# Clustered attention with two MLP layers: exponentials kept in PSUM, fp16 halves made from there, one more buffer each, a lag of three

## The chip, the cores and the metric

The kernel runs on one core of one Trainium2 chip. The metric is device time in microseconds (us), the median of several runs; less is better. Times of single steps come from one profiled execution.

## The reference

Attention in which a query sees only the keys of its own cluster, then two dense layers. Everything is fp32; the core of it:

```python
q_assign = np.argmax(np.einsum('bhsd,hcd->bhsc', q_n, c_n), axis=-1)
k_assign = np.argmax(np.einsum('bhsd,hcd->bhsc', k_n, c_n), axis=-1)
mask = q_assign[:, :, :, None] == k_assign[:, :, None, :]
scores = scale * np.matmul(q, k.transpose(0, 1, 3, 2))
scores = np.where(mask, scores, -1000000000.0)
attn = np.exp(scores - np.max(scores, axis=-1, keepdims=True))
attn = attn / (np.sum(attn, axis=-1, keepdims=True) + 1e-09)
x = np.matmul(attn, v)          # then (B * S, H * D)
h = x @ w1_in;  x = (h * (1.0 / (1.0 + np.exp(-h)))) @ w1_out
h = x @ w2_in;  out = (np.maximum(h, 0.0) + alpha * np.minimum(h, 0.0)) @ w2_out
```

The sizes: batch 2, 8 heads, 768 positions, head width 64, 16 clusters; 1536 tokens, model width 512, inner width 2048.

## The kernel before, in words

**Number format.** Matmuls run in fp16 with three products each: every operand is a sum of a high and a low fp16 half (hi x hi, hi x lo, lo x hi). So each intermediate is split into two halves by a copy to fp16 and a subtraction. The same holds for the weights W1 and W2 (layer 1 and layer 2, each with an `in` and an `out` matrix), which arrive as 64-bit floats, are rebuilt as fp32 from their two 32-bit words and then scaled and split (`to_f32`, `split`, lines 566 to 609), in pieces of 1 MB, on VectorE, ScalarE and GpSimd together.

**Units.** Attention is cut into 96 units: 12 tiles of 128 query rows times 8 heads. Unit `u` has two parts. `front(u)` (line 448) makes the scores of one head for 128 rows against 768 keys: four TensorE matmuls (L458 for the cluster mask, L462 for q times k) into one PSUM score tile `s` of two banks; there are two such tiles (`ps_s`, bufs=2). VectorE takes the row maximum (L474) and two tiny steps (L477, L478). ScalarE takes the exponential with the row sum (L480) into an SBUF buffer `p` of fp32 (a ring of two, `p_buf`), copies it to the high fp16 half (L487), and VectorE subtracts to get the low half (L489). `front_t(u)` (line 493) issues a DMA transpose (L495) of both halves from SyncE's queue (two buffers of halves, `o_hl`; three of transposed halves, `o_pt`, `NPT`). `back(u)` (line 497) multiplies the transposed halves by V: 18 short TensorE matmuls (L507) that add into the PSUM tile `x`, which holds all heads of a query tile. When a tile's eight heads are done, `x_done` (line 520) normalizes, splits and transposes it (L538).

**Order of the work.** `attention()` (line 719) is a generator that emits unit after unit: `front(u)`, then `back(u - LAG)` with `LAG = 2`, then `front_t(u)`, and between them preparation of the next tile's queries (`prep_q_a`, `prep_q_b`), of the second batch's keys and values (from unit 40 on), and background tasks that convert W1. Layer 1 (`layer1`, line 804) runs in seven chunks of one or two tiles. For each chunk the generator is advanced to the unit in `UNITS_BY_CHUNK = (32, 53, 64, 69, 98, 98, 98)` in equal steps between layer 1's steps: 16 first-product groups (L834: 12 matmuls, then tanh L840, L841, copy L844, subtraction L845) and 16 second-product groups (L865). When the generator has made all `NU + LAG` steps, `w2_start` emits the loads and conversions of W2, which reuse the memory of the keys, values and attention buffers. Layer 2 (`layer2`, line 929; L937, L946, L947, L950, L951, L968) follows in three column blocks. A list scheduler then decides the order of each engine's instructions from these priorities, from dependences and from free buffers, so the order below is not simply the program text. Each engine runs its own queue strictly in that order.

The lines of the loop that the change touches:

```python
o = p_buf()
nc.scalar.activation(
    out=view(o, F32, 2, hs), in_=sc[:, :, :hs], func=ACTF.Exp, scale=scl, bias=bias,
    accum_out=sums[n % 2][:, h:h + 1],
)
p = view(o, F32, S)
hl = view(o_hl + 3 * KB * i, F16, 2, S)
nc.scalar.activation(out=hl[:, 0], in_=p, func=ACTF.Copy)
```

The names in rows: `arena` is the one SBUF region in which nearly everything lies, `s` a score tile, `x` the attention output in PSUM, `w` and `m` PSUM tiles of the layers, `stat` small columns.

## Time and profile before

| | us |
|---|---|
| median of 3 runs | 877.86 |
| lowest and highest | 873.18, 877.96 |
| the profiled execution, own time | 873.64 |
| its span in the trace | 871.5 |
| TensorE busy (share of the span) | 704.7 (81%) |
| VectorE busy | 607.4 (70%) |
| ScalarE busy | 468.5 (54%) |
| GpSimd busy | 153.5 (18%) |

Engines in rows: PE is TensorE (PEld its weight loads), DVE VectorE, ACT ScalarE, POOL GpSimd, SP SyncE, which issues the DMAs. `L489` is line 489 of the kernel. Busy time counts an instruction's whole span; in the slices a digit is the busy share in tenths, one slice being a fortieth of the span. A wait is put down to the instruction whose end released it. PEclk is the granted share of TensorE's clock.

### The profile page before, as it was taken

How to read it: one execution, taken by the hardware profiler on the slowest of the kernel's cores; microseconds unless marked ns; L12 is line 12 of the kernel's file. 1: busy time of each engine (PE TensorE's matmuls, PEld its weight loads, DVE VectorE, ACT ScalarE, POOL GpSimd, SP SyncE). 2: the span in 40 equal slices, each digit the busy share in tenths (PEclk: the TensorE clock that was granted, in tenths of full speed). 3: DMA queues.
4: the chain of work that ended last, by engine and by line, in shares of the span. 5: the costliest groups of instructions: out<-in, count | busy, mean ns of one | idle time of the engine just before them, and what ended most of it. 6: DMA issues, size and time to landing. Idle time of an engine off the chain costs nothing.

```text
span 871.5 us, 16209 instructions
## 1 busy us (share of the span) xinstructions
PE 704.7 (81%) x6484; PEld 487.1 (56%) x6484; DVE 607.4 (70%) x1302; ACT 468.5 (54%) x861; POOL 153.5 (18%) x117
## 2 busy tenths in 40 slices
PE   2435267777887997899898869789969999999998
PEld 1323146675766776788677758667424444444443
DVE  6999988888967777875986777786993058206700
ACT  7837576647857664755765577868541023002200
POOL 5734520340201220000000004341190000000000
PEclk9995567689999999999999999999999999999999
DMA  9999878659896786784778687353100000000000
GB/s 278 235 229 249 252 177 134 122 118 163 143 173 115 119 166 98 138 140 73 123 123 139 118 222 177 116 201 139 48 1 13 24 13 1 13 25 12 1 25 25
DMA packets 241595, 101.86 MB, mean 117 GB/s; under 512 B 217328, under 2 KB 227568, under 8 KB 241392
## 3 DMA queue, kind: packets, MB, share of 16 engines
q1 hardware_dynamic: 241520, 100.83, 54.0%
q8 instruction: 51, 0.84, 0.4%
q14 instruction: 24, 0.20, 0.1%
HBM read 44.08 MB, written 3.15 MB: 54 GB/s over the span
## 4 chain that ended last, share of the span: by engine, by line
PE 36%; DMA 12%; DVE 10%; ACT 4%; issue 2%; POOL 1%; SPq 0%; POOLq 0%; DVEq 0%; ACTq 0%
PE w L968 10%; DMA arena<-arena 8%; PE w L937 6%; PE m L968 5%; PE m L937 4%; PE w L865 3%; PE w L834 3%; DMA arena<-in_moe_w_out_dram 2%; PE x L507 2%; DMA arena<-in_moe_w_in_dram 2%; DVE arena L583 1%; DVE arena L586 1%; PE s L458 1%; PE s L462 1%; DVE arena L951 1%
## 5 line engine op out<-in xcount | busy, mean ns | idle before, releaser
L834 PEld LDWEIGHTS <-arena 128*128 128x128 f16 x1344 | 126.6, 107 | 35.1 <-issue 18.8
L834 PE MATMUL w<-arena 128*128 128x256 f16 (+1 forms) x1212 | 137.5, 273 | 10.6 <-DVE arena L841 8.5
L507 PE MATMUL x<-arena 128*128 128x64 f16 x1728 | 75.0, 202 | 79.9 <-DMA arena<-arena 78.9
L865 PEld LDWEIGHTS <-arena 128*128 128x128 f16 x1344 | 118.5, 100 | 20.7 <-POOL arena L605 2.9
L865 PE MATMUL w<-arena 128*128 128x256 f16 (+1 forms) x1200 | 123.9, 260 | 5.4 <-POOL arena L605 2.5
L507 PEld LDWEIGHTS <-arena 128*128 128x128 f16 x1728 | 66.2, 104 | 95.4 <-DMA arena<-arena 91.8
L489 DVE TENSOR_TENSOR arena<-arena 128x768 f16<-128x768 f32 x96 | 95.0, 991 | 32.3 <-ACT arena L487 32.0
L474 DVE TENSOR_REDUCE stat<-s 128x1 f32<-128x768 f32 x96 | 91.1, 951 | 28.4 <-PE s L462 28.2
L480 ACT ACTIVATE arena<-s,stat 128x768 f32<-128x768 f32 x96 | 94.5, 985 | 26.3 <-DVE stat L478 25.5
L487 ACT ACTIVATE arena<-arena 128x768 f16<-128x768 f32 x96 | 80.5, 842 | 42.0 <-DMA arena<-arena 41.0
L937 PEld LDWEIGHTS <-arena 128*128 128x128 f16 x576 | 57.0, 99 | 80.0 <-issue 15.5
L968 PEld LDWEIGHTS <-arena 128*128 128x128 f16 x576 | 56.4, 98 | 68.0
L580 POOL TENSOR_SCALAR arena<-arena 128x1024 f32<-128x1024 f32 x28 | 43.2, 1541 | 287.2 <-DMA arena<-in_moe_w_in_dram 219.1
L937 PE MATMUL w<-arena 128*128 128x512 f16 x384 | 87.7, 383 | 5.3 <-DVE arena L947 5.3
L458 PE MATMUL s<-arena 80*128 80x384 f16 x192 | 69.8, 364 | 17.6 <-DMA arena<-arena 11.1
L968 PE MATMUL w<-arena 128*128 128x512 f16 x384 | 83.9, 379 | 0.0
L950 ACT ACTIVATE arena<-arena,stat 128x512 f16<-128x512 f32 x48 | 34.5, 720 | 88.2 <-DVE arena L947 86.2
L462 PE MATMUL s<-arena 128*128 128x384 f16 x192 | 69.8, 364 | 0.0
L840 ACT ACTIVATE arena<-w,stat 128x256 f32<-128x256 f32 (+1 forms) x101 | 43.5, 434 | 29.3 <-PE w L834 24.2
L583 DVE SCALAR_TENSOR_TENSOR arena<-arena 128x1024 int32<-128x1024 int32 x32 | 42.9, 1340 | 22.1 <-ACT arena L572 8.3
L946 DVE TENSOR_SCALAR arena<-w,stat 128x512 f32<-128x512 f32 x32 | 24.0, 749 | 46.9 <-PE w L937 46.5
L845 DVE SCALAR_TENSOR_TENSOR arena<-arena 128x256 f16<-128x256 f32 (+1 forms) x112 | 49.7, 451 | 6.0 <-ACT arena L844 5.9
(137 smaller groups left out, 1014.1 us busy)
## 6 DMA issues: line engine op xcount, KB each, us to landing
arena<-in_moe_w_in_dram SPq DMA_DIRECT2D x16, 1024.0 KB, 5.9
arena<-in_moe_w_out_dram SPq DMA_DIRECT2D x16, 1024.0 KB, 5.1
arena<-in_k_dram SPq DMA_DIRECT2D x8, 384.0 KB, 3.8
arena<-in_q_dram SPq DMA_DIRECT2D x6, 512.0 KB, 4.9
arena<-in_v_dram SPq DMA_DIRECT2D x8, 384.0 KB, 5.8
out_dram<-arena SPq DMA_DIRECT2D x12, 256.0 KB, 2.0
arena<-arena SPq DMA_TRANSPOSE x149, 3.9
arena<-in_moe_alpha_dram SPq DMA_DIRECT2D x1, 1024.0 KB, 4.7
```

The source lines that it names most:

```text
L458: nc.tensor.matmul(out=sc[:, j, :hs], lhsT=qt2[0:D + C, h], rhs=kt2[0:D + C, h % 2, j * hs:(j + 1) * hs], start=True, stop=False,)
L462: nc.tensor.matmul(out=sc[:, j, :hs], lhsT=qt1[:, h], rhs=kt1[:, h % 2, j * hs:(j + 1) * hs], start=False, stop=True,)
L474: nc.vector.tensor_reduce(out=nm, in_=sc[:, :, :hs], axis=AX.XY, op=ALU.max, negate=True)
L480: nc.scalar.activation(out=view(o, F32, 2, hs), in_=sc[:, :, :hs], func=ACTF.Exp, scale=scl, bias=bias, accum_out=sums[n % 2][:, h:h + 1],)
L487: nc.scalar.activation(out=hl[:, 0], in_=p, func=ACTF.Copy)
L489: en.tensor_tensor(out=hl[:, 1], in0=p, in1=hl[:, 0], op=ALU.subtract)
L507: nc.tensor.matmul(out=x_ps[0][:, h], lhsT=pt[:, ph * T + t], rhs=vt[:, h % 2, t, vh], start=(i == 0), stop=(i == 3 * T - 1),)
L583: nc.vector.scalar_tensor_tensor(out=lo, in0=hi, scalar=3, in1=lo, op0=ALU.logical_shift_left, op1=ALU.bitwise_or)
L834: nc.tensor.matmul(out=hp, lhsT=wi[:, a, kd, f % 2 * 128:f % 2 * 128 + 128], rhs=mov(bb, kd), start=(i == 0), stop=(i == 3 * KD - 1),)
L865: nc.tensor.matmul(out=acc, lhsT=wo[:, a, f % 2, dt * 128:(dt + 1) * 128], rhs=g[:, f, bb], start=(i == 0), stop=(i == 3 * KF - 1),)
L937: nc.tensor.matmul(out=hp, lhsT=in_piece(o_a + 24 * KB, f // 2)[:, a, kd, f % 2 * 128:][:, :128], rhs=x[bb][:, kd], start=(i == 0), stop=( ...
L968: nc.tensor.matmul(out=acc, lhsT=g[:, f, a, t * 128:(t + 1) * 128], rhs=out_piece(o_w, f // 2)[:, bb, f % 2], start=(i == 0), stop=(i == 3 ...
```

## The change

The exponential overwrites the scores in their PSUM tile; the ring `p` is gone. The copy to the high half and the subtraction for the low half read the exponentials from PSUM. The memory of `p` goes to a third buffer of halves (`NHL = 3`) and a fourth of transposed halves (`NPT = 4`). `LAG` is 3. The table `P_LO_DVE`, which had given every subtraction to VectorE, goes, and VectorE keeps them all. `UNITS_BY_CHUNK` stays, so its 98 is now one less than `NU + LAG`.

```diff
--- before.py
+++ after.py
@@ -37,7 +37,6 @@
 V_SCALE_ON = ("papa", "appp")
 SPLIT = ("dddddddd", "dddbdddb", "dbdbdbdb", "dccdcbbc")
 EXP_ON = ("pppppppp", "pppppppp", "appppapp", "papapppp")
-P_LO_DVE = range(96)
 
 MASK = 2.0 ** 15
 BIT23 = 2.0 ** 23
@@ -77,7 +76,8 @@
     NC2 = 3
     N2 = NTILE * 128 // NC2
 
-    NPT = 3
+    NPT = 4
+    NHL = 3
     NSTAT = 464
     NSCR = 192
 
@@ -124,8 +124,7 @@
     o_qraw = region(4 * KB)
     o_kvraw = region(8 * KB)
     o_preq = region(4 * KB)
-    o_p = region(6 * KB)
-    o_hl = region(6 * KB)
+    o_hl = region(NHL * 3 * KB)
     o_pt = region(NPT * 3 * KB)
     o_xf = region(2 * KB)
     o_xhl = region(2 * KB)
@@ -229,9 +228,6 @@
         i = ring_pos.get(name, 0)
         ring_pos[name] = i + 1
         return i % n
-
-    def p_buf():
-        return o_p + 3 * KB * ring("p", 2)
 
 
     half = small_p.tile([128, 12], F32, name="half")
@@ -476,22 +472,19 @@
         )
         nc.vector.tensor_scalar(scl, nm, 2.0 ** 29, d[:, pr:pr + 1], op0=ALU.is_lt, op1=ALU.mult)
         nc.vector.tensor_scalar(bias, nm, scl, None, op0=ALU.mult)
-        o = p_buf()
+        p = sc[:, :, :hs]
         nc.scalar.activation(
-            out=view(o, F32, 2, hs), in_=sc[:, :, :hs], func=ACTF.Exp, scale=scl, bias=bias,
+            out=p, in_=p, func=ACTF.Exp, scale=scl, bias=bias,
             accum_out=sums[n % 2][:, h:h + 1],
         )
-        p = view(o, F32, S)
-        i = u % 2
-        hl = view(o_hl + 3 * KB * i, F16, 2, S)
+        hl = view(o_hl + 3 * KB * (u % NHL), F16, 2, 2, hs)
         nc.scalar.activation(out=hl[:, 0], in_=p, func=ACTF.Copy)
-        en = nc.vector if u in P_LO_DVE else nc.gpsimd
-        en.tensor_tensor(out=hl[:, 1], in0=p, in1=hl[:, 0], op=ALU.subtract)
+        nc.vector.tensor_tensor(out=hl[:, 1], in0=p, in1=hl[:, 0], op=ALU.subtract)
         pt = view(o_pt + 3 * KB * (u % NPT), F16, 2 * T, 128)
         pt_of[u] = pt
 
     def front_t(u):
-        hl = view(o_hl + 3 * KB * (u % 2), F16, 2 * S)
+        hl = view(o_hl + 3 * KB * (u % NHL), F16, 2 * S)
         nc.sync.dma_start_transpose(out=pt_of[u], in_=hl)
 
     def back(u):
@@ -711,7 +704,7 @@
                 f()
 
 
-    LAG = 2
+    LAG = 3
     NU = NTILE * H
     ready = set()
     g1_done = set()
```

The scheduler gives another order. First VectorE late in attention, amid the first product of a layer-1 chunk, before: the subtractions (L489) of units 69 and 70 and the reductions (L474) of units 71 and 72.

```order
L841 SCALAR_TENSOR_TENSOR arena<-arena,w 128x256
L489 TENSOR_TENSOR arena<-arena 128x768
L474 TENSOR_REDUCE stat<-s 128x1
L416 SCALAR_TENSOR_TENSOR arena<-arena,stat 128x8x64
L423 COPY arena<-arena 128x8x64
L477 TENSOR_SCALAR stat<-stat 128x1
L841 SCALAR_TENSOR_TENSOR arena<-arena,w 128x256
L845 SCALAR_TENSOR_TENSOR arena<-arena 128x256
L474 TENSOR_REDUCE stat<-s 128x1
L478 TENSOR_SCALAR stat<-stat 128x1
L468 TENSOR_SCALAR stat<-stat 128x4
L489 TENSOR_TENSOR arena<-arena 128x768
```

Now, at the corresponding place: the subtractions of units 68 and 69 and the reduction of unit 70 (lines have moved: L470 is the reduction, L482 the subtraction, L834 and L838 the layer-1 pair, L473 and L474 the tiny steps).

```order
L482 TENSOR_TENSOR arena<-s,arena 128x768
L474 TENSOR_SCALAR stat<-stat 128x1
L834 SCALAR_TENSOR_TENSOR arena<-arena,w 128x256
L838 SCALAR_TENSOR_TENSOR arena<-arena 128x256
L470 TENSOR_REDUCE stat<-s 128x1
L838 SCALAR_TENSOR_TENSOR arena<-arena 128x256
L834 SCALAR_TENSOR_TENSOR arena<-arena,w 128x256
L473 TENSOR_SCALAR stat<-stat 128x1
L482 TENSOR_TENSOR arena<-s,arena 128x768
L474 TENSOR_SCALAR stat<-stat 128x1
L834 SCALAR_TENSOR_TENSOR arena<-arena,w 128x256
L838 SCALAR_TENSOR_TENSOR arena<-arena 128x256
```

Before, a subtraction stands behind the reduction of the unit two later; now behind that of the unit one later, and one reduction lies between two subtractions instead of two.

The second place is VectorE where the scale of W1's `out` matrix is set (L682; L675 now), which the first L865 waits for; these are the rows before it, before.

```order
L489 TENSOR_TENSOR arena<-arena 128x768
L164 TENSOR_SCALAR stat<-stat 128x1
L474 TENSOR_REDUCE stat<-s 128x1
L845 SCALAR_TENSOR_TENSOR arena<-arena 128x128
L167 TENSOR_SCALAR stat<-stat 128x1
L682 TENSOR_SCALAR stat<-stat 128x8
L477 TENSOR_SCALAR stat<-stat 128x1
L474 TENSOR_REDUCE stat<-s 128x1
```

And now.

```order
L470 TENSOR_REDUCE stat<-s 128x1
L280 TENSOR_SCALAR arena<-arena 128x8x16
L838 SCALAR_TENSOR_TENSOR arena<-arena 128x128
L473 TENSOR_SCALAR stat<-stat 128x1
L159 TENSOR_SCALAR stat<-w 128x1
L474 TENSOR_SCALAR stat<-stat 128x1
L163 TENSOR_SCALAR stat<-stat 128x1
L166 TENSOR_SCALAR stat<-stat 128x1
L482 TENSOR_TENSOR arena<-s,arena 128x768
L675 TENSOR_SCALAR stat<-stat 128x8
```

Before, it stands behind the reduction of unit 22 and the subtraction of unit 20; now behind the reduction of unit 17 and the subtraction of unit 16.

The third place is SyncE's queue at the end of attention: transposes of the last units (L495; L488 now), the last x (L538; L531), the loads of W2 (L561; L554) and of alpha (L889; L882), before.

```order
L538 DMA_TRANSPOSE arena<-arena 128x8x128
L561 DMA arena<-in_moe_w_in_dram 128x4x512
L495 DMA_TRANSPOSE arena<-arena 128x12x128 x2
L889 DMA arena<-in_moe_alpha_dram 128x2048
L561 DMA arena<-in_moe_w_in_dram 128x4x512
L495 DMA_TRANSPOSE arena<-arena 128x12x128 x2
L561 DMA arena<-in_moe_w_in_dram 128x4x512
L495 DMA_TRANSPOSE arena<-arena 128x12x128 x2
L561 DMA arena<-in_moe_w_in_dram 128x4x512
L538 DMA_TRANSPOSE arena<-arena 128x8x128
```

And now.

```order
L488 DMA_TRANSPOSE arena<-arena 128x12x128 x2
L554 DMA arena<-in_moe_w_in_dram 128x4x512
L488 DMA_TRANSPOSE arena<-arena 128x12x128 x2
L882 DMA arena<-in_moe_alpha_dram 128x2048
L554 DMA arena<-in_moe_w_in_dram 128x4x512
L488 DMA_TRANSPOSE arena<-arena 128x12x128
L554 DMA arena<-in_moe_w_in_dram 128x4x512
L488 DMA_TRANSPOSE arena<-arena 128x12x128
L531 DMA_TRANSPOSE arena<-arena 128x8x128
L554 DMA arena<-in_moe_w_in_dram 128x4x512 x5
```

Six unit transposes stand behind the first W2 load before, four now; the loads of W2 stand among them in both.

## Rows read from the trace of the kernel before

**Rows 1.** The page, busy tenths in 40 slices of the span, two engines.
```profile
PE   2435267777887997899898869789969999999998
...
DVE  6999988888967777875986777786993058206700
```

**Rows 2.** Busy time by stretch; columns in the first line.
```profile
core 0: us, PE busy (x) PEld busy (x) DVE busy (x) ACT busy (x) POOL busy (x), PEclk, DMA share, GB/s
50.00:168.00 118.00, 65.51 (x715) 51.17 (x716) 107.52 (x241) 76.13 (x140) 34.61 (x20) 0.68 0.90 205
168.00:508.00 340.00, 288.41 (x3708) 239.56 (x3706) 262.54 (x652) 219.36 (x438) 35.77 (x23) 0.96 0.74 129
508.00:655.00 147.00, 122.24 (x934) 88.21 (x932) 121.34 (x189) 99.22 (x172) 55.43 (x32) 0.97 0.41 128
```

**Rows 3.** Timeline (start us, length us), TensorE: the first layer-1 output.
```profile
167.97 0.61 PE L865 MATMUL w<-arena 128*128 128x128 f16 x4
```

**Rows 4.** The chain that ended last, 380 to 400 us: start, length.
```profile
385.42 0.53 PE x L507 x18
...
391.80 7.86 PE w L865 x72
```

**Rows 5.** Who waited for whom, 168 to 508 us: total us, times, longest.
```profile
PE x L507 <- DMA arena<-arena: 34.9, 31, 2.6
ACT arena L487 <- DMA arena<-arena: 30.6, 22, 3.2
DVE arena L489 <- ACT arena L487: 28.5, 28, 3.4
...
PE s L458 <- ACT arena L480: 1.1, 3, 0.6
```

**Rows 6.** Single lines: count, ns min/median/max, first and last start (us).
```profile
L489 DVE TENSOR_TENSOR arena<-arena x96: 939/954/2875, 45.4 to 523.2; 128x768 f16<-128x768 f32 x96
...
L841 DVE SCALAR_TENSOR_TENSOR arena<-arena,w x101: 270/410/423, 120.7 to 583.8; 128x256 f32<-128x256 f32 x69, 128x128 f32<-128x128 f32 x32
...
L845 DVE SCALAR_TENSOR_TENSOR arena<-arena x112: 234/417/1734, 123.2 to 585.4; 128x256 f16<-128x256 f32 x80, 128x128 f16<-128x128 f32 x32
...
L458 PE MATMUL s<-arena x192: 322/327/528, 29.7 to 508.7; 80*128 80x384 f16 x192
```

**Rows 7.** Groups by shape: xcount, busy us, mean ns, idle before (us).
```profile
L489 DVE TENSOR_TENSOR arena<-arena 128x768 f16<-128x768 f32 x96 | 95.0, 991 | 32.3 <-ACT arena L487 32.0
...
L474 DVE TENSOR_REDUCE stat<-s 128x1 f32<-128x768 f32 x96 | 91.1, 951 | 28.4 <-PE s L462 28.2
...
L923 ACT ACTIVATE arena<-arena,stat 128x512 f16<-128x512 f32 x12 | 7.6, 706 | 0.0
...
L974 ACT ACTIVATE arena<-w,stat 128x512 f32<-128x512 f32 x8 | 5.5, 687 | 69.5 <-PE w L968 69.5
```

**Rows 8.** Timeline around unit 81: its scores, subtraction, scores of 83, its `back`.
```profile
450.55 0.33 PE L458 MATMUL s<-arena 80*128 80x384 f16 x1
450.72 0.33 PE L462 MATMUL s<-arena 128*128 128x384 f16 x1
...
455.23 0.96 DVE L489 TENSOR_TENSOR arena<-arena 128x768 f16<-128x768 f32 x1
...
455.95 0.33 PE L458 MATMUL s<-arena 80*128 80x384 f16 x1
...
460.37 0.70 PE L507 MATMUL x<-arena 128*128 128x64 f16 x18 [0.46 <-DMA arena<-arena]
```

**Rows 9.** Timeline around unit 70: its scores, scores of 72, subtraction, `back`.
```profile
406.20 0.33 PE L458 MATMUL s<-arena 80*128 80x384 f16 x1
...
413.19 0.33 PE L458 MATMUL s<-arena 80*128 80x384 f16 x1
...
415.71 0.95 DVE L489 TENSOR_TENSOR arena<-arena 128x768 f16<-128x768 f32 x1
...
420.81 0.70 PE L507 MATMUL x<-arena 128*128 128x64 f16 x18
```

## The prediction

> **What bounds the kernel now.** I read the page's slices first, then the busy time by stretch, then who waits for whom inside the long middle stretch, then single rows. The slices [rows 1] show three regimes: VectorE nearly full in the first fifth, TensorE at 7 to 9 tenths in the middle, TensorE alone at the end (9 in almost every slice of the last quarter). By stretch [rows 2]: from 50 to 168 us VectorE is busy 107.5 of 118 us, 91% (it turns W1 into fp16 beside the first heads). From 168 us, where the first layer-1 output matmuls start [rows 3], to 508 us, where the last score is made [rows 6], TensorE is busy 288.4 of 340 us and idle 51.6. From 508 to 655 us W2 is loaded and converted: VectorE 121.3 of 147, TensorE 122.2. What follows 655 us is not touched by the change and can only start earlier.
>
> In the middle stretch TensorE's largest wait is `back` (L507) waiting for a transpose: 34.9 us in 31 waits [rows 5]. The same transposes hold the fp16 copy L487 for 30.6 us (its buffer of halves is still being read), and L487 holds the subtraction L489 for 28.5 us. VectorE is there only 77% busy (262.5 of 340, [rows 2]). So the middle is a latency loop, score to transposed halves, laid over engines that are each nearly full. The change lengthens one buffer of that loop and shortens another.
>
> **The change part by part.**
>
> *The three passes.* The exponential (L480) writes PSUM in place of SBUF, the copy (L487) reads PSUM, and the subtraction (L489) reads one PSUM operand. L489 has a median of 954 ns but a worst case of 2875 [rows 6]; its mean is 991 ns [rows 7]. The step with one PSUM operand, L841, is steady (270/410/423 for its shortest, median and longest), the one with two SBUF operands, L845, again has a tail (234/417/1734) at nearly the same median. So I put L489 at 950 ns: 96 x 41 ns = 3.9 us less, mostly in the first 200 us, where GpSimd works beside it; bounds 0 and twice that (8 us). L487: the nearest row from PSUM is L974, 687 ns, against L923, 706, from SBUF, both 512 wide [rows 7]; 96 x 19 ns = 1.8 us, on ScalarE, which has room (219 of 340 us in the middle): 0 on the path. No row shows ScalarE writing PSUM; by the same two rows I bound L480 at 19 ns either way and take 0.
>
> [...]
>
> *A third buffer for halves, a fourth for transposed halves.* They take away most of L487's 30.6 us of waiting, and of L489's 28.5 behind it. None of that is on TensorE itself; it counts only as shorter latency from score to transpose.
>
> *The scores are held longer.* There are two score tiles. Before, `front(u+2)` could write when the exponential of u was done; now only when its subtraction is done. Unit 81 [rows 8]: scores at 450.55, subtraction done at 456.19, scores of unit 83 at 455.95, so these would be 0.2 us late. Unit 70 [rows 9]: scores at 406.20, subtraction done at 416.66, scores of unit 72 at 413.19: 3.5 us late. Behind a waiting score on TensorE stand layer-1 matmuls and the next `back`; VectorE's reduction L474 waits for it. From score to end of subtraction these two units take 5.6 and 10.5 us, and the hold binds when that exceeds two unit times. 96 units between 29.7 and 508.7 us [rows 6] are 5.0 us each: at 5.6 it is free, at 10.5 it is not. Part of the 10.5 is running ahead itself (an early score waits in VectorE's queue), and a score made later waits less; I take 7, nearer to unit 81, and cost the hold at nothing. Its cover is that slack between 7 and 10; with the cover gone it is the second rival.
>
> *The lag of three.* The order does not do what the number says. Counting rows on TensorE, `back(u)` stands behind the scores of 2.8 later units on average before, and of 2.2 now, because scores can no longer run ahead (the order on VectorE shows why: the subtraction of unit 70 stands behind the reduction of unit 72 before, that of unit 69 behind the reduction of unit 70 now). Prices: the matmuls of a score 0.164 us apart (0.66 for four), `back` 0.53 us, a layer-1 matmul 7.86/72 = 0.109 us [rows 4, 8]. By these there are 12.0 us of TensorE work between `front(u)` and `back(u)` before and 10.2 now, from unit 16 on. Needed, from score to landing: 9.8 us at unit 81 (450.55 to the `back` at 460.37 that had waited for it), at most 14.6 at unit 70 (to 420.81). With the copy's wait gone and the queues shorter I take 11.0, nearer to unit 81: 0.8 us short, once per loop of 3.2 units, 0.25 us a unit. For the 77 units scored or finished after the first layer-1 output that is 19 us in place of 34.9; the ends are 0 us and, with 14.6, more than now.
>
> *What moves.* W1's last scale (L682) stands on VectorE behind 21 subtractions and 23 reductions before, behind 17 and 18 now: 4 x 0.99 + 5 x 0.95 = 8.7 us of work less in front [rows 7], at 91% busy 10 us, so layer-1 output starts at 158 us. Those units come later: 5 x 0.66 + 4 x 0.53 = 5.4 us of TensorE. And ahead of the last score stand 1152 and 1034 layer-1 matmuls (first and second product) where 1104 and 960 stood: 122 x 0.109 = 13.3 us. On SyncE the first W2 load still stands between the last transposes (four are behind it, six before), and the other loads wait, as now, for the last scores that read the keys; so W2 starts with the last score as today, although the program text emits it one chunk later (attention now has 99 steps where the table's last entries say 98).
>
> *The sum.* The middle starts at 158; TensorE's work 288.4 + 5.4 + 13.3 = 307; waits for transposes 19; its other idle time 51.6 - 34.9 = 17 as before: last score at 501, 8 us earlier (508.7). In the W2 stretch 13.3 us of TensorE work and four pieces of 0.8 us on VectorE (L841 and L845, one for each twelve of the 48 matmuls) are gone, of engines 83% busy; between 0 and 8 us of it shows, and I take 4. Total 12 us: 873.6 - 12 = 862 us. That is against the profiled execution (span 871.5, own time 873.64); the median of the runs shown is 877.86, 0.5% above it, a spread that the range allows for. Differences of about 1% can be told from no change.
>
> **The rivals.**
>
> *The waits only change place (no change).* The transposes set the pace, as many and as long, and `back` now has less work ahead of it (10.2 us against 12.0). For it: 31 waits in the middle [rows 5], the smaller distance. Against: the copy's own wait on the transposes goes. If the 34.9 us stay: 862 + 16 = 878 us.
>
> *The hold becomes the wait (slower).* Place: L458, waiting for the subtraction two units back. It decides once score to subtraction takes more than two unit times. Price: the mean lead of the two units shown is 1.9 us for two units, 0.95 a unit; over the 74 units scored after 168 us, 70 us if none were absorbed. With a third of it left, 23 us: 885 us. For it: unit 70, and in-order queues in which a subtraction stands behind layer-1 steps. Against: unit 81, and that a later score queues less. In the kernel before, a score waited for its exponential 3 times in the middle, 1.1 us in all [rows 5], so the trace shows room and not the price. [...]
>
> *The waits vanish (faster still).* If score to landing falls below 10.2 us, as at unit 81, the 19 us go too: 843 us.
>
> **How the numbers follow.** Forecast 862 us: 0.43. Waits stay, 878: 0.24. Hold binds, 885: 0.23. Waits vanish, 843: 0.10. About 0.08 of the forecast's weight ends less than 1% from now, and the rest of it with the last case makes faster 0.45; same 0.31 and slower 0.24 follow from the two others. The likeliest case alone, with L489 between 0 and 8 us and the W2 stretch between 0 and 8, spans 851 to 869. The range goes from just under the case without waits, 838, to just over the hold, 888.
>
> **What would show it.** Right: L489 near 950 ns without a tail; the copy's wait on transposes under 10 us; `back` waiting 15 to 25 us in the middle; the first layer-1 output near 158 us and the last score near 501. Wrong: scores (L458) waiting for L489 by more than 15 us in all; `back` waiting 35 us or more; W2 taking longer than 147 us from the last score to the full TensorE.

## The result and the profile after

The changed kernel took 887.92 us (median of 4 runs, 886.41 to 888.50) against 877.91 of the kernel before: ratio 1.0128, 95% interval 1.0104 to 1.0152. A second comparison, beside experiments, gave 1.0141 (1.0100 to 1.0181). It is slower, where 862 us was predicted; it lies just under the upper end of the stated range of 838 to 888 us, on the other side of the kernel before. The profiled execution took 886.41 us, span 884.5 us, 13.0 more than before.

The line numbers move: scores L458/L462 are now L454/L458, the reduction L474 is L470, the exponential L480 is L476, the copy L487 is L481, the subtraction L489 is L482, `back` L507 is L500, the layer-1 products L834/L865 are L827/L858.

The slices of the page, TensorE and VectorE, as [rows 1]:

```profile
PE   2344267777799977988897987699768999999998
...
DVE  6999988876688777776866877766996048306700
```

Busy time by stretch; the cuts are the first layer-1 output (153.7 us, 168.0 before), the last score (525.7, 508.4 before), the first layer-2 output (672.5, 659.5 before). It answers to [rows 2]:

```profile
core 0: us, PE busy (x) PEld busy (x) DVE busy (x) ACT busy (x) POOL busy (x), PEclk, DMA share, GB/s
50.00:154.00 104.00, 52.55 (x626) 39.74 (x626) 93.92 (x216) 69.45 (x128) 30.45 (x21) 0.99 0.86 215
154.00:526.00 372.00, 312.96 (x3924) 259.30 (x3922) 280.05 (x694) 230.15 (x465) 32.39 (x22) 0.93 0.71 125
526.00:672.00 146.00, 115.35 (x817) 78.35 (x815) 115.78 (x175) 96.51 (x159) 53.30 (x32) 0.92 0.40 125
```

The middle begins 14 us earlier, as W1 is done sooner, and lasts 372 us instead of 340: TensorE is idle 59.0 us there instead of 51.6 and has 24.5 us more to do. The W2 stretch is 4 us shorter, but TensorE, which lost work there, is idle 30.6 of its 146 us instead of about 25. The PEclk of the first row (0.99, and 0.68 in [rows 2]) is not used here: in that stretch many score matmuls take 0.53 us in both traces (the one at 80.77 us below is one), against 0.33 later.

Who waited on TensorE, from 30 to 154 us and from 154 to 526 us (us in all, times, longest), as [rows 5]:

```profile
PE s L454 <- DVE arena L482: 32.2, 6, 11.1
PE x L500 <- DMA arena<-arena: 14.7, 10, 4.0
```

```profile
PE x L500 <- DMA arena<-arena: 38.0, 31, 3.3
PE w L858 <- DVE arena L587: 5.2, 5, 1.8
PE s L454 <- DVE arena L482: 3.3, 7, 0.7
```

A wait that was not there before leads the W1 stretch: scores stand 32.2 us for the subtraction two units back. In the middle this wait is only 3.3 us, while `back` still waits for its transposes, 31 times as before and 38.0 us instead of 34.9 (19 were predicted). The passes themselves came out cheaper, by group of the page (xcount, busy us, mean ns, idle before) and, for the subtraction, by its single line (ns shortest/median/longest), as [rows 6, 7]:

```profile
L476 ACT ACTIVATE s<-s,stat 128x768 f32<-128x768 f32 x96 | 92.0, 959 | 61.8 <-DVE stat L474 56.6
...
L482 DVE TENSOR_TENSOR arena<-s,arena 128x768 f16<-128x768 f32 x96 | 91.2, 951 | 14.4 <-ACT arena L481 13.6
...
L481 ACT ACTIVATE arena<-s 128x768 f16<-128x768 f32 x96 | 77.2, 807 | 1.0
```

```profile
L482 DVE TENSOR_TENSOR arena<-s,arena x96: 899/950/959, 45.5 to 534.0; 128x768 f16<-128x768 f32 x96
```

The subtraction has lost its tail (959 ns at most, 2875 before); the copy no longer waits for a transpose (1.0 us of idle time).

The longest of the six waits that make up the 32.2 us, on the timeline (start, length, in brackets the idle time before and who ended it), TensorE and then VectorE around 80 to 100 us:

```profile
80.77 0.53 PE L458 MATMUL s<-arena 128*128 128x384 f16 x1
85.33 1.14 PE L500 MATMUL x<-arena 128*128 128x64 f16 x18 [4.03 <-DMA arena<-arena]
...
87.93 0.59 PE L427 MATMUL m<-arena 128*128 128x16 f16 x16
99.58 0.48 PE L454 MATMUL s<-arena 80*128 80x384 f16 x1 [11.06 <-DVE arena L482]
```

```profile
82.88 0.95 DVE L470 TENSOR_REDUCE stat<-s 128x1 f32<-128x768 f32 x1
...
85.09 0.95 DVE L470 TENSOR_REDUCE stat<-s 128x1 f32<-128x768 f32 x1
...
92.61 2.20 DVE L576 SCALAR_TENSOR_TENSOR arena<-arena 128x1024 int32<-128x1024 int32 x1 [1.49 <-POOL arena L573]
...
94.99 1.27 DVE L587 SCALAR_TENSOR_TENSOR arena<-arena,stat 128x1024 f16<-128x1024 f32 x1
96.18 2.12 DVE L579 SCALAR_TENSOR_TENSOR arena<-arena 128x1024 int32<-128x1024 int32 x1
...
98.49 0.94 DVE L482 TENSOR_TENSOR arena<-s,arena 128x768 f16<-128x768 f32 x1
```

The score of unit 8 waits 11.06 us for a subtraction that stands on VectorE behind the conversions of W1 (L576, L579, L587). This is the picture on which the first theory was built: that the time is lost here. The experiments show that it is not.

### The profile page after: what moved, and what is told of

Its sections match the earlier page's. It is cut to its first block, busy times and chain, and to the rows that moved or that the text cites. A ratio compares the mean times of both kernels' runs of the same rounds, so it can differ in the third digit from the quotient of the medians.

```text
span 884.5 us, 16213 instructions
## 1 busy us (share of the span) xinstructions
PE 705.3 (80%) x6484; PEld 483.8 (55%) x6484; DVE 603.8 (68%) x1302; ACT 469.1 (53%) x861; POOL 143.8 (16%) x117
## 4 chain that ended last, share of the span: by engine, by line
PE 44%; DMA 22%; DVE 18%; ACT 8%; issue 5%; POOL 2%; SPq 1%; ACTq 0%; DVEq 0%; POOLq 0%
DMA arena<-arena 17%; PE w L961 9%; PE w L858 8%; PE w L930 7%; PE m L961 5%; PE w L827 4%; PE x L500 4%; PE m L930 4%; DMA arena<-in_moe_w_in_dram 2%; DVE arena L482 2%; DVE arena L576 2%; DVE arena L579 2%; DMA arena<-in_moe_w_out_dram 2%; DVE arena L587 2%; PE s L454 2%
## 5 line engine op out<-in xcount | busy, mean ns | idle before, releaser
L827 PE MATMUL w<-arena 128*128 128x256 f16 (+1 forms) x1284 | 142.8, 269 | 10.3 <-DMA arena<-arena 6.7
L827 PEld LDWEIGHTS <-arena 128*128 128x128 f16 x1344 | 122.6, 103 | 35.4 <-issue 15.1
L858 PE MATMUL w<-arena 128*128 128x256 f16 (+1 forms) x1248 | 129.3, 261 | 7.0 <-DVE arena L587 5.2
L858 PEld LDWEIGHTS <-arena 128*128 128x128 f16 x1344 | 118.0, 101 | 23.5 <-DVE arena L587 6.1
L476 ACT ACTIVATE s<-s,stat 128x768 f32<-128x768 f32 x96 | 92.0, 959 | 61.8 <-DVE stat L474 56.6
L470 DVE TENSOR_REDUCE stat<-s 128x1 f32<-128x768 f32 x96 | 91.6, 954 | 41.6 <-PE s L458 38.5
L500 PE MATMUL x<-arena 128*128 128x64 f16 x1728 | 75.9, 201 | 54.7 <-DMA arena<-arena 54.6
L500 PEld LDWEIGHTS <-arena 128*128 128x128 f16 x1728 | 67.1, 103 | 69.9 <-DMA arena<-arena 66.5
L482 DVE TENSOR_TENSOR arena<-s,arena 128x768 f16<-128x768 f32 x96 | 91.2, 951 | 14.4 <-ACT arena L481 13.6
L454 PE MATMUL s<-arena 80*128 80x384 f16 x192 | 70.0, 365 | 37.6 <-DVE arena L482 35.5
L930 PE MATMUL w<-arena 128*128 128x512 f16 x384 | 91.8, 396 | 7.4 <-DVE arena L940 7.4
L573 POOL TENSOR_SCALAR arena<-arena 128x1024 f32<-128x1024 f32 x28 | 41.0, 1465 | 292.4 <-DMA arena<-in_moe_w_in_dram 227.5
L961 PE MATMUL w<-arena 128*128 128x512 f16 x384 | 83.9, 379 | 0.0
L481 ACT ACTIVATE arena<-s 128x768 f16<-128x768 f32 x96 | 77.2, 807 | 1.0
L833 ACT ACTIVATE arena<-w,stat 128x256 f32<-128x256 f32 (+1 forms) x107 | 46.8, 441 | 49.1 <-PE w L827 43.0
L458 PE MATMUL s<-arena 128*128 128x384 f16 x192 | 70.8, 369 | 0.0
L576 DVE SCALAR_TENSOR_TENSOR arena<-arena 128x1024 int32<-128x1024 int32 x32 | 40.8, 1275 | 25.6 <-POOL arena L573 13.1
L834 DVE SCALAR_TENSOR_TENSOR arena<-arena,w 128x256 f32<-128x256 f32 (+1 forms) x107 | 39.7, 374 | 16.1 <-ACT arena L833 15.9
```

The lines of the kernel that those rows point to most:

```text
L454: nc.tensor.matmul(out=sc[:, j, :hs], lhsT=qt2[0:D + C, h], rhs=kt2[0:D + C, h % 2, j * hs:(j + 1) * hs], start=True, stop=False,)
L458: nc.tensor.matmul(out=sc[:, j, :hs], lhsT=qt1[:, h], rhs=kt1[:, h % 2, j * hs:(j + 1) * hs], start=False, stop=True,)
L470: nc.vector.tensor_reduce(out=nm, in_=sc[:, :, :hs], axis=AX.XY, op=ALU.max, negate=True)
L476: nc.scalar.activation(out=p, in_=p, func=ACTF.Exp, scale=scl, bias=bias, accum_out=sums[n % 2][:, h:h + 1],)
L482: nc.vector.tensor_tensor(out=hl[:, 1], in0=p, in1=hl[:, 0], op=ALU.subtract)
L500: nc.tensor.matmul(out=x_ps[0][:, h], lhsT=pt[:, ph * T + t], rhs=vt[:, h % 2, t, vh], start=(i == 0), stop=(i == 3 * T - 1),)
```

## The experiments

In what follows "hold" means that a score tile stays taken until the subtraction that reads it is done, not only until the exponential. "Ahead" is the number of layer-1 matmuls that stand on TensorE before the last score, counted from the order of the program. All ratios are to the kernel before, run on the same chip beside the experiment; the groups of experiments ran on different chips, so kernels of different groups are compared by these ratios. Trace times (last score and what follows it) come from one execution each. The edits are shown shortened: constants are written in for names, and lines that only keep book are left out.

| kernel | units with the hold | lag | ratio (95%) | ahead | last score, us | last score to first layer-2 output, us | TensorE busy in it, us |
|---|---|---|---|---|---|---|---|
| before | none | 2 | 1 | 2064 | 508.4 | 151.1 | 126.0 |
| changed | all | 3 | 1.0128 (1.0104 to 1.0152) | 2186 | 525.7 | 146.8 | 116.1 |
| hold alone | all | 2 | 1.0297 (1.0265 to 1.0330) | 2216 | 540.1 | 144.8 | 111.6 |
| changed, lag two | all | 2 | 1.0263 (1.0216 to 1.0310) | 2216 | 539.3 | 146.7 | 113.2 |
| hold, lag three, old buffers | all | 3 | 1.0163 (1.0108 to 1.0218) | 2186 | 526.9 | 145.4 | 116.0 |
| hold, passes on SBUF | all | 2 | 1.0481 (1.0418 to 1.0544) | 2263 | 552.1 | 145.3 | 106.9 |
| before, lag three | none | 3 | 1.0092 (1.0056 to 1.0128) | 2100 | 510.7 | 152.3 | 124.9 |
| hold from 24 on | 24 to 95 | 3 | 1.0070 (1.0036 to 1.0103) | 2186 | – | – | – |
| hold to 23 | 0 to 23 | 3 | 0.9974 (0.9942 to 1.0006) | 2028 | 500.9 | 155.7 | 132.4 |
| hold to 23, lag two | 0 to 23 | 2 | 1.0032 (0.9989 to 1.0076) | 2064 | 515.0 | 149.2 | 126.4 |
| hold to 23 and from 56 | 0 to 23, 56 to 95 | 3 | 1.0194 (1.0130 to 1.0259) | 2235 | 526.2 | 147.2 | 112.1 |
| hold to 56 | 0 to 56 | 3 | 1.0003 (0.9979 to 1.0027) | 2052 | 512.1 | 152.8 | 127.8 |
| hold to 35 | 0 to 35 | 3 | 1.0083 (1.0053 to 1.0112) | 2052 | 511.0 | 157.7 | 130.4 |

**The parts of the change one by one.** Four kernels take the change apart. The hold alone, on the kernel before (buffers and lag as there):

```diff
-        o = p_buf()
+        p = sc[:, :, :hs]
         nc.scalar.activation(
-            out=view(o, F32, 2, hs), in_=sc[:, :, :hs], func=ACTF.Exp, ...
+            out=p, in_=p, func=ACTF.Exp, ...
```

> The kernel before with one part of the change: the exponential overwrites the scores in PSUM and both halves are made from there; two buffers of halves, three of transposed halves, lag of two as before. Theory 1 (the hold of the score tile until the subtraction costs the time, mostly while VectorE is full with W1): 885 to 895 us, scores waiting for the subtraction by about 35 us in all as in the changed kernel, last score 15 to 20 us later than 508. Theory 2 (the lag of three and the order that it gives cost the time): 874 to 880 us, as before.

Measured: 898.27 us, ratio 1.0297, scores waiting 32.1 us, last score at 540.1. Theory 1 holds, beyond its range of 885 to 895 us, and the hold by itself costs more than the whole change: something else in the change gives back half of it. The changed kernel with a lag of two:

```diff
-    LAG = 3
+    LAG = 2
```

> The changed kernel with a lag of two instead of three; hold and buffers as changed. Theory 1 (hold): 884 to 890 us, scores waiting for the subtraction 30 us or more, last score near 525. Theory 2 (lag): 874 to 880 us, last score near 508.

Measured: 895.40 us, 1.0263, above the ranges of both theories. So the lag of three is what gives back; with a lag of two the extra buffers are all that remains of the change beside the hold, and their effect is within the intervals. The kernel before with a lag of three:

```diff
-    LAG = 2
+    LAG = 3
```

> The kernel before with a lag of three and nothing else: exponentials in SBUF, two buffers of halves, three of transposed halves. Theory 1 (hold): 872 to 880 us, scores waiting for the subtraction not at all, W1's last scale near 165 us. Theory 2 (lag): 884 to 890 us, W1's last scale near 151 us and the last score near 525 as in the changed kernel.

Measured: 881.33 us, 1.0092, between the ranges of the two theories. Without a hold the lag of three costs a little; theory 2 falls, its last score is at 510.7. Hold and lag of three with the old buffers (these two edits on the kernel before, that of the hold and that of the lag):

> Hold and lag of three with the buffers of before (two of halves, three of transposed halves): the changed kernel without its two extra buffers. Theory 1 (with the hold the lag of three gives back 10 to 14 us and the buffers 0 to 4): ratio 1.012 to 1.020. Theory 2 (the lag needs the buffers): 1.024 or more.

Measured: 886.73 us, 1.0163: the changed kernel in all but its buffers, and on TensorE in the very same order. The extra buffers bring nothing that can be measured; the lag of three, under the hold, 1.3%. So the two edits do not add up. With a lag of two the hold costs 3.0%. With a lag of three, which alone costs 0.9%, the hold adds only 0.7% with the old buffers and 0.4 to 0.5% in the changed kernel, and the intervals of these ratios overlap with that of the lag alone. Part of the 1.3% is TensorE's clock. The middle of the two kernels, first the lag of two, then of three:

```profile
core 0: us, PE busy (x) PEld busy (x) DVE busy (x) ACT busy (x) POOL busy (x), PEclk, DMA share, GB/s
154.00:540.00 386.00, 328.01 (x3967) 272.23 (x3966) 284.57 (x693) 231.55 (x466) 33.94 (x23) 0.90 0.69 121
```

```profile
152.00:527.00 375.00, 312.37 (x3926) 258.12 (x3924) 281.66 (x695) 231.61 (x465) 34.59 (x23) 0.94 0.71 124
```

TensorE has 41 matmuls fewer (4.5 us by [rows 4]) but is busy 15.6 us less: the granted clock is 0.94 on the mean instead of 0.90. Busy time per matmul agrees: 82.7 ns with the lag of two (328.01 us for 3967) and 79.6 with the lag of three (312.37 for 3926), 4% apart as the two clocks are. Why they differ, no run here tells.

**The hold without the passes on PSUM.** The kernel before, exponentials in SBUF, with the hold as a wait and nothing else:

```diff
+            if j == 0 and u >= 2:
+                tc.add_manual_dep(mm.ins, sub_of[u - 2].ins.name, ...)
```

> The kernel before, exponentials in SBUF and every pass as it was, with one thing added: the first score matmul of a unit waits until the subtraction two units back is done. So the hold alone, without any pass on PSUM. Theory 1 (the hold is the cause): ratio 1.02 to 1.04, scores waiting for the subtraction 25 us or more, last score 530 or later. Theory 2 (the passes on PSUM, or what they do on the engines, take part of it): under 1.015.

Measured: 915.35 us, 1.0481, scores waiting 44.3 us. Theory 1 holds, beyond its range: with a lag of two the hold is the cause, and the passes on PSUM are not; they take 1.8% off its price (1.0481 against 1.0297). The groups of this kernel, and of the one with hold and passes on PSUM (L488/L480 the exponential, L497/L487 the subtraction, L495/L485 the copy):

```profile
L488 ACT ACTIVATE arena<-s,stat 128x768 f32<-128x768 f32 x96 | 94.5, 985 | 53.9 <-DVE stat L486 45.1 <-DVE stat L167 3.2 <-DVE stat L164 2.7
L497 DVE TENSOR_TENSOR arena<-arena 128x768 f16<-128x768 f32 x96 | 93.0, 976 | 21.9 <-ACT arena L495 21.6
...
L495 ACT ACTIVATE arena<-arena 128x768 f16<-128x768 f32 x96 | 79.7, 840 | 1.8 <-DMA arena<-arena 1.0
```

```profile
L480 ACT ACTIVATE s<-s,stat 128x768 f32<-128x768 f32 x96 | 92.0, 959 | 72.8 <-DVE stat L478 69.4 <-DVE stat L162 1.9 <-DVE stat L160 1.1
...
L487 DVE TENSOR_TENSOR arena<-s,arena 128x768 f16<-128x768 f32 x96 | 91.2, 952 | 20.6 <-ACT arena L485 19.8 <-issue 0.3
...
L485 ACT ACTIVATE arena<-s 128x768 f16<-128x768 f32 x96 | 77.3, 808 | 4.2 <-DMA arena<-arena 3.4
```

On SBUF the three passes take 26, 24 and 32 ns longer on the mean (985, 976 and 840 ns against 959, 952 and 808), and each lengthens the time for which the tile is held. The last line also tells that, with only two buffers of halves, the copy waits just 3.4 us for transposes (41.0 before): the hold spaces the copies, no third buffer is needed for that.

**Where the hold costs: not where it is seen.** The changed kernel with exponentials in SBUF for units 0 to 23 (two buffers of them, two of halves, three of transposed halves in the same 21 KB):

```diff
+        p = view(o_soft + 3 * KB * (u % 2), F32, 2, hs) if u < 24 else sc[:, :, :hs]
         nc.scalar.activation(
-            out=p, in_=p, func=ACTF.Exp, ...
+            out=p, in_=sc[:, :, :hs], func=ACTF.Exp, ...
```

> The changed kernel, but units 0 to 23 keep their exponentials in SBUF (two buffers of them, two of halves, three of transposed halves in the same 21 KB); from unit 24 on as changed, lag three throughout. Theory 1 (hold, and that in the W1 stretch): scores wait for the subtraction less than 8 us in all (35.5 in the changed kernel), W1's last scale near 165, last score near 508, 866 to 876 us. Theory 2 (lag): 884 to 890 us. A third case: the hold costs as much in the later units, then the gain is under 5 us: 882 to 888.

Measured: 882.17 us, 1.0070, the third case: half of the loss is left without the hold in the W1 stretch (only its times are used here). The complement:

```diff
-        p = view(o_soft + 3 * KB * (u % 2), F32, 2, hs) if u < 24 else sc[:, :, :hs]
+        p = view(o_soft + 3 * KB * (u % 2), F32, 2, hs) if u >= 24 else sc[:, :, :hs]
```

> The complement of the run with early units in SBUF: units 0 to 23 as in the changed kernel (exponentials in PSUM, hold), from unit 24 on exponentials in SBUF with two buffers of halves and three of transposed halves; lag three throughout. Theory 1 (the hold costs in both parts, about half in each): ratio 1.004 to 1.010, scores waiting for the subtraction 28 to 35 us, all before 160 us, last score 515 to 522. Theory 2 (the first 24 units are the whole cost, and what is lost there cannot be won back): 1.010 or more. Theory 3 (units after 23 are the whole cost): under 1.003, last score near 508.

Measured: 870.10 us, 0.9974, scores waiting 27.6 us, last score at 500.9. Theory 3 holds, against the picture on the timeline: nearly the whole visible wait is there and the kernel is as fast as the one before. Against the kernel with the same lag and no hold (1.0092) it is even 1.2% faster. In the W1 stretch VectorE is the engine that is full (busy 90.0 us of the 100 from 50 to 150 us in this kernel); it does the conversions while the scores wait, W1's last scale comes at 149 us instead of 166, and what attention lost there layer 1 gains. The same with a lag of two:

```diff
-    LAG = 3
+    LAG = 2
```

> As the run with the hold in units 0 to 23 alone, but with a lag of two. Account A (early hold brings W1 forward by 12 us at no cost, and without the hold behind it a lag of three costs, as it does in the kernel before): ratio 0.985 to 0.994, last score 492 to 500. Account B (the early hold needs the lag of three, as the hold throughout did): ratio 1.004 or more.

Measured: 877.94 us, 1.0032. Account A falls, and the value is just under B's: with a hold at the start, too, a lag of three is if anything the better one.

The changed kernel itself was run again beside the next group:

> The changed kernel once more, beside the others of this group on the same chip: a ratio of 1.010 to 1.015 to the kernel before, as in its first comparison. Both theories.

Measured: 887.29 us, 1.0141.

**Order or hold.** From unit 24 on scores hardly wait in the trace, but the order differs: 456 layer-1 matmuls stand ahead of score 24 in the changed kernel, 208 before. (The kernel with the hold to 23 has 456 as well and loses nothing, so it is not this place alone.) Three kernels set the order by hand, with an order-only dependency of a layer-1 matmul on a score or the reverse:

```diff
+                    if f == 0 and i == 0 and c in A_AFTER:
+                        issue_after(mm, score_at[A_AFTER[c]])
```

The changed kernel in the order of before:

> The changed kernel with the order on TensorE of the kernel before: each chunk's first products and outputs of layer 1 are issued behind the score behind which they stood there (208 instead of 456 layer-1 matmuls ahead of score 24, 2052 instead of 2186 ahead of the last). Theory 1 (the loss is the order: layer-1 matmuls let ahead of scores, which comes back nowhere because the end follows the last score by 357 to 366 us in every run so far): last score back near 510, 868 to 877 us, ratio below 1.003. Theory 2 (the hold itself takes the time, and layer 1 only fills it): TensorE waits where layer 1 stood, scores wait for the subtraction 45 us or more instead of 35, last score 520 or later, ratio 1.008 or more.

The kernel before in the order of the changed one:

> The kernel before with the order on TensorE of the changed kernel: eleven scores are issued behind the chunk starts of layer 1 that stand ahead of them there (2197 layer-1 matmuls ahead of the last score instead of 2064); exponentials in SBUF, no hold, lag two. Theory 1 (order): last score 518 to 528, ratio 1.010 to 1.020. Theory 2 (hold): at most the 133 matmuls by 0.109 us, 14 us later at the last score but given back behind it, ratio below 1.006.

The changed kernel in the order of the one with the hold to 23:

> The changed kernel, hold throughout, with layer 1 issued from score 29 on behind the scores behind which it stands in the run with the hold in units 0 to 23 alone (2088 layer-1 matmuls ahead of the last score instead of 2186). Order theory (the hold costs because it lays layer 1 ahead of the scores): last score 503 to 512, ratio 0.996 to 1.005. Hold theory (scores two units on can't be written earlier whatever stands behind them): scores wait for the subtraction 15 us or more behind 160 us, last score 518 or later, ratio 1.009 or more.

Measured: 904.17 us (1.0334, last score 540.4), 902.94 us (1.0329, last score 546.0), 897.43 us (1.0290, last score 530.2). All three are some 3% behind the kernel before, the second further than its theory 1 allowed. In the first, scores wait 51.9 us in all, as theory 2 has it; in the third, TensorE from 154 to 530 us reads

```profile
PE x L505 <- DMA arena<-arena: 47.3, 35, 3.2
PE s L458 <- DVE arena L487: 11.2, 12, 2.6
```

with 11.2 us of scores waiting for the subtraction instead of 3.3 (15 were expected), and `back` 47.3. So the theory that the order alone is the loss falls: under the hold the scores can't be made as early as without it, and layer 1 put ahead of them fills time that would be idle. That is why the middle of the changed kernel shows almost no wait of scores. The second speaks for the order theory all the same: without any hold, scores put late in the order cost as much. And all three were fixed by hand; no kernel was run whose own order was fixed in this way, so what the fixing costs by itself is not known.

**Where the filling can't be paid back.** Two pairs of kernels have the same order on TensorE to the scores of unit 57 and differ only in the last 39 or 40 units, in the hold and the buffers and passes that go with it. Hold to 23 and from 56 on (exponentials in SBUF `if 24 <= u < 56`), against hold to 23 (`if u >= 24`):

> Hold in units 0 to 23 and from 56 on; exponentials of units 24 to 55 in SBUF. Lag three. If the hold costs in the last 40 units: ratio 1.009 to 1.016, last score 518 or later. If it costs in units 24 to 55: 0.994 to 1.003, last score near 503. Spread evenly: 1.003 to 1.009.

Measured: 891.45 us, 1.0194 against 0.9974, more than its range gave the last 40 units. Hold to 56 (in SBUF `if u >= 57`), against the changed kernel (1.0128 and 1.0141):

> Hold in units 0 to 56; exponentials of units 57 to 95 in SBUF; lag three. 2052 layer-1 matmuls stand ahead of the last score (2186 in the changed kernel, 2028 with the hold in units 0 to 23 alone). If what counts is the work left for TensorE behind the last score: last score 503 to 512, W2 stretch 150 to 157 us, ratio 0.996 to 1.006. If the units 24 to 56 pay for the hold themselves: last score 514 or later, ratio 1.010 or more.

Measured: 875.57 us, 1.0003. At its switch unit 57's halves overwrite unit 56's transposed halves, so that unit 56 gets a wrong sum; the amount of work is the same, but `back` of 56 now follows the halves of 57 and comes at 379.6 us, against 370.4 in the changed kernel. Busy time from unit 56 to the last score and from there to the first layer-2 output: hold to 23; hold to 23 and from 56; hold to 56; the changed kernel.

```profile
349.00:501.00 152.00, 132.99 (x1620) 107.15 (x1618) 118.83 (x290) 98.54 (x192) 0.00 (x0) 0.99 0.74 131
501.00:657.00 156.00, 132.71 (x998) 95.63 (x996) 123.37 (x195) 104.65 (x178) 55.63 (x32) 0.93 0.38 122
```

```profile
347.00:526.00 179.00, 159.63 (x1843) 131.25 (x1840) 129.03 (x306) 106.94 (x212) 0.00 (x0) 0.95 0.68 116
526.00:673.00 147.00, 111.84 (x768) 75.60 (x769) 118.94 (x178) 96.33 (x158) 55.08 (x32) 0.88 0.38 124
```

```profile
360.00:512.00 152.00, 132.39 (x1590) 108.16 (x1588) 114.93 (x273) 95.25 (x184) 0.00 (x0) 0.97 0.74 130
512.00:665.00 153.00, 128.00 (x974) 91.88 (x973) 121.67 (x192) 102.92 (x176) 56.39 (x32) 0.96 0.40 123
```

```profile
358.00:526.00 168.00, 147.89 (x1737) 121.33 (x1736) 123.76 (x289) 101.05 (x199) 0.00 (x0) 0.95 0.70 121
526.00:672.00 146.00, 115.35 (x817) 78.35 (x815) 115.78 (x175) 96.51 (x159) 53.30 (x32) 0.92 0.40 125
```

With the hold these 40 units take 179 and 168 us, without it 152 and 152. TensorE is idle for 19 to 20 us in each of the four; it does 223 and 147 matmuls more with the hold, 207 and 134 of them layer 1 laid between the scores (the table's "ahead"). Behind the last score those matmuls are missing: TensorE is busy 112 and 115 us instead of 133 and 128, and the stretch is only 9 and 7 us shorter. It takes 145 to 147 us in every kernel of the table in which TensorE has 107 to 116 us to do there. In these the conversion of W2 starts with the last score and its last step ends 137 to 142 us behind it; that it sets the length of the stretch is argued from this and not tested by a run. Two of the kernels with the order set by hand do not fit: 140 us, and 142 with TensorE busy 124. Of 27 and 16 us lost, 18 and 9 remain by these cuts; the starts differ by 2 us, and the ends of the stretch by 16 and 7.

How it looks, TensorE's timeline in the changed kernel and in the one with the hold to 23:

```profile
436.71 0.34 PE L454 MATMUL s<-arena 80*128 80x384 f16 x1 [0.42 <-DVE arena L482]
...
437.38 1.47 PE L827 MATMUL w<-arena 128*128 128x256 f16 x12
...
439.25 2.67 PE L858 MATMUL w<-arena 128*128 128x256 f16 x23 [0.28 <-DVE arena L834]
...
441.84 0.33 PE L454 MATMUL s<-arena 80*128 80x384 f16 x1
```

```profile
425.43 0.33 PE L458 MATMUL s<-arena 80*128 80x384 f16 x1
...
426.10 0.63 PE L504 MATMUL x<-arena 128*128 128x64 f16 x16
426.56 0.33 PE L458 MATMUL s<-arena 80*128 80x384 f16 x1
```

In the changed kernel 35 layer-1 matmuls stand between two scores. Without the hold the next score follows 1.13 us behind the first, with only the rest of a `back` between them.

**Checks of this account.** The kernel before with the sixth chunk's first products behind the last score, so with less filling:

```diff
+                    if i == 0 and c == 5:
+                        issue_after(mm, score_at[95])
```

> The kernel before with all first products of the sixth chunk of layer 1 issued behind the last score: 1920 layer-1 matmuls ahead of it instead of 2064, at once a test whether the last score sets the end. Theory 1: last score 10 to 16 us earlier (144 x 0.109 us = 15.7, less what TensorE then waits), end 4 to 14 us earlier, ratio 0.985 to 0.996. Theory 2 (TensorE's total work and its waits decide): no change or slower, ratio 0.998 to 1.01.

Measured: 882.26 us, 1.0073. The last score came 3.7 us earlier, the stretch behind it took 165.9 us instead of 151.1, TensorE busy 145.5. So the last score does not set the end by itself: in the kernels of the table and this one, from about 116 us of TensorE work upward, the stretch grows with that work. Then W2 emitted as early as before:

```diff
-UNITS_BY_CHUNK = (32, 53, 64, 69, 98, 98, 98)
+UNITS_BY_CHUNK = (32, 53, 64, 69, 99, 99, 99)
```

> The changed kernel with the last three entries of the table of units by chunk at 99 instead of 98, so that the program emits W2's conversion right behind attention, as before, and not a chunk later. The prediction's step (W2 starts with the last score anyway): ratio 1.010 to 1.018 as the changed kernel, the small sums (L210) waiting for ScalarE's squares behind the last score still 6 us or more. The rival (the later emission costs, by these sums standing in TensorE's queue): those waits under 2 us, ratio 1.000 to 1.008.

Measured: 889.43 us, 1.0197, just above the range of the prediction's step, and the small sums still wait 9.3 us; the later place in the program text costs nothing. The hold to 35 (`if u >= 36`):

> Hold in units 0 to 35; exponentials of units 36 to 95 in SBUF; lag three; 2052 layer-1 matmuls ahead of the last score. If what counts is the work left for TensorE behind the last score: ratio 0.994 to 1.004, last score 500 to 510. If the units 24 to 56 pay for the hold themselves: between that and the run with the hold to 56.

Measured: 883.20 us, 1.0083, last score 511.0. The account would have it near the hold to 23 or to 56, and it is 0.8% slower than the second. The hold to 55 (`if u >= 56`), with the switch one unit before that of the hold to 56:

> Hold in units 0 to 55; exponentials of units 56 to 95 in SBUF. Lag three. If the hold costs in the last 40 units: ratio 0.994 to 1.003, last score near 503. If it costs in units 24 to 55: 1.009 to 1.016. Spread evenly: 1.003 to 1.009.

Measured: 888.50 us, 1.0178. This speaks against the account: its last 40 units have no hold, and it is as slow as the changed kernel. At its switch unit 56's transposed halves overwrite unit 55's, so that unit 55 gets a wrong sum and its `back` comes 6 us later than in the changed kernel (369.6 us, 363.5). That does not explain the time, for the scores of unit 60 are made at 370.2 us, before those of the kernel with the hold to 56 (376.4), in which the overwriting delays `back` by more. Its last score comes at 516.0 us, 10 us before that of the changed kernel, but from there to the first layer-2 output it takes 157.2 us instead of 146.8. TensorE there:

```profile
528.89 7.83 PE L861 MATMUL w<-arena 128*128 128x256 f16 x55
536.55 0.69 PE L503 MATMUL x<-arena 128*128 128x64 f16 x18
537.08 15.12 PE L861 MATMUL w<-arena 128*128 128x256 f16 x137
552.03 0.69 PE L503 MATMUL x<-arena 128*128 128x64 f16 x18
```

The last `back` stands behind 192 layer-1 matmuls and starts 36 us behind the last score, 18 us in the kernel with the hold to 56. Whether this place in the order is the whole loss was not tested. Between the hold from 24 on (1.0070) and no hold at all, both with a lag of three (1.0092), there is no difference either. So the late hold costs 2.2% and 1.3% in the two pairs that begin as the changed kernel does, nothing against the hold to 55, and nothing measurable where the units before 24 had no hold. Each such edit also changes the order and the buffers from its unit on; the kernels with the hold to 35, 55 and 56 alone lie 1.7% apart, which stays unexplained and is as much as the price itself.

## Why the prediction was wrong

**The passes: right.** The subtraction was put at 950 ns and has a mean of 951; its tail is gone. The copy gained 35 ns a piece (842 to 807; 19 were taken), the exponential 26 (985 to 959; 0 taken). By the medians the subtraction takes 950 ns with one PSUM operand and 954 without [rows 6].

**The buffers: right in what is seen, wrong in the reason.** The copy's wait went from 30.6 us in the middle [rows 5] to nothing. But with two buffers and the hold it is 3.4 us in the whole span (41.0 before): the hold removes it. In the kernel with the hold to 23, whose later units have two buffers and no hold, it is 25.8 us.

**The hold, costed at nothing: the step that made the sign wrong.** The 7 us from score to subtraction came out: 7.7 us over units 22 to 47 and 7.1 over units 56 to 91 (end of L482 less start of the unit's first score, means). But they came out with the hold in force, which has made the scores late; that they are below two unit times tells nothing of its price. The test was to be made on the kernel before, where scores run free, and in one stage at a time instead of with 5.0 us from all 96 units. From unit 56 to 91 the kernel before makes a unit in 4.15 us (340.3 to 485.4 us over 35), two in 8.3, and there the time from score to subtraction is 9.2 us on the mean (12.2 against 8.8 in units 22 to 47): its scores ran ahead of the subtraction by 1.1 us at the median (by 2.8 in units 22 to 47), and the hold forbids just that. Units 81 and 70 [rows 8, 9] were two samples where the mean of all was to be had. What the runs showed in place of nothing: 3.0% for the hold alone with a lag of two, and 0.4 to 0.7% beside a lag of three.

**The lag of three: given no price of its own.** The prediction priced it only through the transposes. Alone it costs 0.9%; under the hold it gives back 1.3%.

**Waits for transposes, 34.9 to 19 us: the step that failed by most.** They are 38.0, in 31 waits as before. Score to landing was put at 11.0 us and is on the mean 12.1 (units 22 to 47) and 11.3 (56 to 91), against 10.2 us of work between: short by 1 to 2 us, not 0.8. The first rival had this part: as many waits and as long. But in the kernel with the hold to 23 they are 38.1 us as well and its time is that of before, so the wait is as long in a kernel that loses nothing. Left at its old size the prediction's sum gives 878 us, no change. From there to 886 are 3 us more of this wait and the three terms of the next paragraph; no run parts these 8 us into hold and lag.

**What moves: right in the parts, and it did not help.** W1's last scale came 15 us earlier, the first layer-1 output at 153.7 (158 predicted); the 122 layer-1 matmuls stand where they were counted (2186 less 2064); the W2 stretch shrank by 4 us, as taken. By the prediction's own sum: start 4.3 us earlier than forecast, TensorE's work 313.0 instead of 307 (+6), waits for transposes 38 instead of 19 (+19), other idle time 21 instead of 17 (+4): the last score 25 us later than forecast, at 526 instead of 501, and the rest as forecast. The 13.3 us of layer-1 work put ahead of the last score and the 4 us that the stretch behind it returned were both in the sum, so these 9 us of loss were foreseen; the gains that were to outweigh them did not come. (A slip without weight: by the prediction's own cases its last two chances are 0.32 and 0.23, not 0.31 and 0.24.)

**The rivals.** The second rival gave 885 us, near the 886.41 of the profiled execution, and named the mechanism, but it looked for its price in scores that wait, a third of 70 us; that its number is so near is luck. Its sign ("scores waiting for L489 by more than 15 us in all", 35.5 measured) came true, in a stretch where the wait is free (the kernel with the hold to 23); in the later units the hold shows only as layer-1 matmuls between scores. A hold throughout cost time in the two kernels that have it alone (1.0297 and 1.0481), a hold in units 0 to 23 none that can be measured (0.9974).

**What stays open:** why the lag of three helps under the hold and costs without it, in which units from 24 on the hold costs, how much of the loss is the order that the scheduler gives rather than the hold itself, and the 1.7% by which kernels with the hold to 35, 55 and 56 differ.

## What to carry to other kernels

Where a buffer is to be held longer, take from the kernel before, stage by stage, the time from the write to the later reader, and compare it with the time per unit of that stage times the number of buffers: where it is longer, the producer runs ahead of that reader now, and the hold will delay it. Whether the delay costs is a second question: in units 0 to 23 the scores ran ahead by 4.6 us at the median, and the hold there was free. A wait that can be seen can cost nothing, as in the W1 stretch, where VectorE was the full engine (90.0 of 100 us), and a delay filled with other work shows no wait at all; ask of the filling work whether the place it was taken from can do without it (here the W2 stretch hardly can: it lasts 145 us even when TensorE has 107 us to do in it). Two edits that each cost can cost less together, as hold and lag do here, so each is to be run alone and with the other. The exponential and both halves are cheaper with PSUM here (959, 807 and 951 ns on the mean against 985, 842 and 991), so the form with the hold for early units alone is worth a trial, but here it is no faster than the kernel before beyond its interval.

## What the runs showed of the hardware

The clock: two kernels with 41 matmuls between them in the middle differ by 15.6 us of busy time there, 11 more than the matmuls explain, at a granted clock of 0.90 and 0.94. ScalarE writes its exponential to PSUM in 959 ns on the mean and to SBUF in 985, 128 x 768 from PSUM in both; it copies 128 x 768 to fp16 from PSUM in 807 ns and from SBUF in 842 (the kernel before). VectorE's subtraction took 899 to 959 ns with one operand in PSUM (the changed kernel), and 939 to 2875 with both in SBUF (the kernel before).
